# A new order for the first part of a Performer + FNet kernel: three strings that hold the order, the PSUM banks and the matmul tile forms

## The chip, the cores and the metric

One core of one Trainium2 chip. The metric is the device time of one execution in microseconds, the median of several runs. The core's engines are TensorE (PE, with its weight loads PEld), VectorE (DVE), ScalarE (ACT), GpSimd (POOL) and SyncE (SP), which here only issues DMAs. Each engine takes its instructions in the order in which the program lists them and waits on semaphores for what others have to do first.

## The reference

Two layers in a row, cut to what matters:

```python
def phi(x):                                   # q, k: (8, 8, 576, 64), omega: (128, 64)
    proj = np.einsum('bhsd,md->bhsm', x, omega)
    h = proj - np.sum(x * x, axis=-1, keepdims=True) / 2.0
    return np.exp(h - np.max(h, axis=-1, keepdims=True)) / np.sqrt(m)
q_p, k_p = phi(q * scale), phi(k * scale)
kv = np.einsum('bhsm,bhsd->bhmd', k_p, v)
z = np.sum(k_p, axis=2)
num = np.einsum('bhsm,bhmd->bhsd', q_p, kv)
den = np.einsum('bhsm,bhm->bhs', q_p, z)[..., None] + 1e-06
x = (num / den)                               # as (8, 576, 512)

u = x + np.real(np.fft.fft(np.fft.fft(x, axis=1), axis=2))
un = (u - mean(u)) / np.sqrt(var(u) + 1e-06)
out = u + np.maximum(un @ w_ch1, 0.0) @ w_ch2 # w_ch1: (512, 2048), w_ch2: (2048, 512)
```

## The kernel before, in words

**Two parts.** The first part runs the attention of all 8 batches, the Fourier mix, the residual and the conversion of the weights, and in between the plain form of the MLP for the first four blocks of tokens ("plain" blocks 0 to 3). The second part runs the MLP of all other tokens in a form with fewer multiplications, for which it needs sums of weight blocks and of token blocks made beforehand. Everything that the change touches lies in the first part.

**What the first part consists of.** Attention goes by 32 pairs of heads, n = 0 to 31, four to a batch. For each: k and q are loaded (`loads`, L497 and L501) and v (L506); PE transposes them (L642, `kqT`); PE makes the scores (`pairs`, L737); DVE takes the maximum (L679), ACT the exponent (L696); PE multiplies with v (L772, `kv`); PE transposes q's features (L642, `qeT`); PE makes numerator and denominator (L820, L828), and DVE or ACT divides (L833 to L849), which gives `x`. When four pairs of a batch are done, `mix` folds x (DVE or POOL, L873 to L915) and multiplies it with the tables cs and sn (L939, L953), ACT keeps `y` (L969), and PE multiplies it with cd and sd (L999, L1010). `residual` and `summed` (L1044 to L1066) add x and store u (L1080, L1035). The weights are loaded as `raw` (L596) into one of four slabs and converted by POOL, DVE and ACT (`narrow`, L562 to L582).

**The plain blocks** load u (`norm_of`, L1103 with its step at L1193), normalize it (DVE L1222 to L1224, POOL L1226, DVE L1228), transpose it on PE (L1233), copy it (ACT L1237, `unT`), and run the two matmuls (`plain_of`, L1299 with its step at L1287, sixteen of them, fc0 to fc15; the hidden values leave by `hidden`, L1278 to L1283; then L1324 with its step at L1309, eight of them) and store (L1334 to L1342, `rest`).

**What the first part makes for the second.** `w2_parts` (L1532 to L1579) makes the sums of w2 in seven groups, in the order 1, 2, 3, 5, 6, 4, 7. A group has four additions into the tile `sums`, the later groups four more before them into `big` (L1550, on POOL or DVE), and then five DMAs on SP that store it (L1573, L1575). A group's additions come behind the stores of the one before, by the semaphores of the same tiles. `weight_sums` (L1622 to L1628) does w1, `block_norms` (L1453 to L1484) normalizes the four blocks of tokens of the second part's first batch, i = 0 to 3, through the same `norm_of`, and adds them up (tiles `tt`, `unT`); the first matmul that reads `tt` is at L1794.

**How the order comes about.** Each of these functions is a stream (a generator) that yields a `Step` ahead of each few instructions. The step says which engines may do it, which buffers and PSUM banks it takes and gives, and what must have been listed before it. `Listing.run` holds the streams' next steps in a list, and at each turn places one of them: its instructions are emitted then and there, so the order of the turns is the order on every engine's queue. Which one is placed, and on which of its engines, is read from the string `PICKS` (one character or more for each turn). Each bank that a step takes is read from `BANKS`, and each matmul step asks `form()` for its tile form, a letter code from `FORMS` (one tile of 128 rows, or two or four tiles of 64 or 32 rows and columns beside each other). The scheduling is manual: nothing reorders the instructions afterwards.

**The chains run ahead.** Nine more pieces of work are no steps: `ahead` (L1640 to L1676) normalizes blocks of tokens for the later batches of the second part, nine chains (0 to 8) of a load on SP (L1109), statistics on ACT (L1662, L1665), three small operations on POOL (L1667 to L1669), a scaling on ACT (L1671), a transpose on DVE (L1674) and a store on SP (L1676). They go in by `BETWEEN`: after so many placed steps of the first part, such a chain is taken on by one piece. `go_on` and the planner's own search in `Listing.run` know nothing of their durations.

**Two further steps that matter below**: `warm` (L607 to L611) lets PE run six matmuls on a zeroed tile while the first loads are under way, and `first` (L617 to L622) transposes omega, which the ACT queue loads (L518), and scales it; the first scores need it.

The lines of the loop in which the order is read, and the call:

```python
        while todo:
            other, n = next(picks, (None, None))
...
            while between and between[0][0] == placed:
                next(between.pop(0)[1], None)
...
    listing.run(
        [first(), loads(), loads_v(), load_tables(), frames(), plain_norms(), mixing()]
        + [pairs(i) for i in range(NS)]
        + [w2_parts(), weight_sums(), block_norms(0, mlpp), plain(), weights(), warm()],
        picked(PICKS, 1),
        BANKS,
        betweens(BETWEEN),
    )
```

## Time and profile before

| | us |
|---|---|
| median of 3 runs | 1116.88 (1119.11, 1116.88, 1114.37) |
| the profiled execution's own time | 1114.35 |
| its span in the trace | 1112.6 |
| first part's last step on PE ends | 418.4 |
| PE busy in the span | 1093.4 |
| granted clock of PE | 1.00 |

The profiled execution is as fast as the fastest of the three runs, and its span lies 1.75 us below its own time. PE's first part ends where the program's eight last matmul steps at L1324 end and a short instruction at L2367 begins (418.37); a dozen microseconds before it everything that PE still has to do in the first part is these matmuls. How busy the engines are, stretch by stretch, and what PE waited for, is shown with the prediction.

### The profile page before, as it was taken

What the parts mean: (1) busy time and instruction counts of PE and PEld (TensorE: products, weight loads), DVE (VectorE), ACT (ScalarE), POOL (GpSimd) and SP (SyncE); (2) the same over time, 40 slices, a digit from 0 to 9 for tenths busy, and PEclk for the clock granted to TensorE, in tenths of its full rate; (3) what the DMA queues carried; (4) which work ended last, traced back from release to release, by engine and by line L of the source; (5) the groups of instructions that cost most, each with busy time, mean ns of one, the idle gap of its engine ahead of it and who ended that gap; (6) DMA issues with size and microseconds to landing.
All of it is one profiled execution on the core that took longest, in us unless ns stands there. A gap on an engine that the chain in (4) does not pass through costs nothing.

```text
span 1112.6 us, 41751 instructions
## 1 busy us (share of the span) xinstructions
PE 1093.4 (98%) x17507; PEld 934.7 (84%) x17507; DVE 885.9 (80%) x1685; ACT 539.1 (48%) x1644; POOL 390.4 (35%) x404
## 2 busy tenths in 40 slices
PE   8999999999999999999999999999999999999998
PEld 6788888878869666799998888998667999667998
DVE  6999999996676766688697777898667898668895
ACT  6998898856635464624214453223563223341221
POOL 2343443644473346634513455000365000152000
PEclk9999999999999999999999999999999999999999
DMA  7856767575675668798898768757678757556553
GB/s 230 229 183 182 241 182 220 162 212 160 221 231 187 188 169 314 236 300 287 247 303 300 211 200 260 213 155 237 206 216 262 220 154 223 167 158 220 151 158 113
DMA packets 196588, 236.77 MB, mean 213 GB/s; under 512 B 53808, under 2 KB 120624, under 8 KB 196400
## 3 DMA queue, kind: packets, MB, share of 16 engines
q1 hardware_dynamic: 195904, 233.83, 68.7%
q8 instruction: 138, 2.26, 0.9%
q14 instruction: 50, 0.41, 0.1%
q10 hardware_dynamic: 496, 0.26, 0.1%
HBM read 182.13 MB, written 56.10 MB: 214 GB/s over the span
## 4 chain that ended last, share of the span: by engine, by line
PE 90%; ACT 4%; DVE 3%; DMA 2%; issue 1%; SPq 0%; POOL 0%; DVEq 0%; ACTq 0%
PE banks L2247 30%; PE banks L1794 27%; PE banks L642 5%; PE banks L737 5%; PE banks L1324 5%; PE banks L1299 4%; PE banks L1946 4%; PE banks L772 3%; PE banks L820 2%; ACT e L696 2%; PE banks L999 1%; PE banks L939 1%; DMA kq<-in_q_dram 1%; DVE nmx L679 1%; PE banks L953 1%
## 5 line engine op out<-in xcount | busy, mean ns | idle before, releaser
L2247 PE MATMUL banks<-wl,sums 128*64 128x128 f32 x3584 | 217.5, 273 | 0.1
L2247 PEld LDWEIGHTS banks<-wl,sums 128*64 128x64 f32 x3584 | 201.6, 137 | 2.1 <-issue 0.5
L696 ACT ACTIVATE e<-banks,nmx 128x128 f32<-128x128 f32 x576 | 164.3, 426 | 21.8 <-DVE nmx L679 20.8
L679 DVE TENSOR_REDUCE nmx<-banks 128x8 f32<-128x1024 f32 (+1 forms) x96 | 89.3, 951 | 18.5 <-PE banks L737 15.4
L2247 PE MATMUL banks<-wl,hid 128*64 128x128 f32 x1536 | 99.0, 273 | 0.5 <-DVE part L2222 0.5
L2247 PEld LDWEIGHTS banks<-wl,hid 128*64 128x64 f32 x1536 | 88.0, 137 | 1.8 <-DVE part L2222 0.7
L1794 PE MATMUL banks<-unw,wxw 128*64 128x256 f32 x704 | 86.2, 379 | 0.0
L2217 ACT ACTIVATE s<-banks 128x128 f32<-128x128 f32 x112 | 30.9, 277 | 109.8 <-PE banks L2247 109.8
L737 PE MATMUL banks<-om,kqT 64*64 64x128 f32 (+1 forms) x1804 | 80.1, 276 | 2.5 <-issue 1.1
L737 PEld LDWEIGHTS banks<-om,kqT 64*64 64x64 f32 (+1 forms) x1804 | 66.2, 148 | 13.0 <-issue 4.8
L2247 PE MATMUL banks<-wl,hx 128*64 128x128 f32 x1152 | 73.6, 273 | 0.4 <-DVE part L2222 0.4
L1794 PEld LDWEIGHTS banks<-unw,wxw 128*64 128x64 f32 x704 | 53.3, 137 | 22.0
L1794 PE MATMUL banks<-rx,wxw 128*64 128x256 f32 x576 | 71.7, 379 | 0.0
L1794 PE MATMUL banks<-ttw,wxw 128*64 128x256 f32 x576 | 70.6, 379 | 0.0
L1819 ACT ACTIVATE s<-banks 128x512 f32<-128x512 f32 x65 | 38.5, 596 | 64.9 <-PE banks L1794 59.8
L2247 PEld LDWEIGHTS banks<-wl,hx 128*64 128x64 f32 x1152 | 65.4, 137 | 1.2 <-DVE part L2222 0.6
L1299 PE MATMUL banks<-unT,w 128*64 128x128 f32 (+1 forms) x720 | 64.7, 276 | 1.8 <-DVE qeT L656 1.8
L582 POOL TENSOR_TENSOR w<-w,raw 128x512 f32<-128x512 f32 x28 | 37.7, 1357 | 77.4 <-DVE raw L576 74.5
L2296 POOL TENSOR_TENSOR more<-more,part 128x512 f32<-128x512 f32 x2 | 2.7, 1336 | 172.8 <-ACT part L2289 172.8
L1299 PEld LDWEIGHTS banks<-unT,w 128*64 128x64 f32 (+1 forms) x720 | 58.6, 160 | 5.3 <-issue 2.3
L1794 PEld LDWEIGHTS banks<-rx,wxw 128*64 128x64 f32 x576 | 44.0, 137 | 17.6
L1794 PEld LDWEIGHTS banks<-ttw,wxw 128*64 128x64 f32 x576 | 44.0, 137 | 17.6
(289 smaller groups left out, 2413.3 us busy)
## 6 DMA issues: line engine op xcount, KB each, us to landing
wl<-w2l SPq DMA_DIRECT2D x245, 256.0 KB, 3.9
wxw<-w1x SPq DMA_DIRECT2D x120, 256.0 KB, 3.2
raw<-in_moe_w_ch_dram SPq DMA_DIRECT2D x32, 512.0 KB, 5.3
kq<-in_k_dram SPq DMA_DIRECT2D x32, 288.0 KB, 4.4
kq<-in_q_dram SPq DMA_DIRECT2D x32, 288.0 KB, 4.7
vd<-in_v_dram SPq DMA_DIRECT2D x32, 288.0 KB, 5.5
ur<-us SPq DMA_DIRECT2D x30, 256.0 KB, 4.6
w2l<-sums SPq DMA_DIRECT2D x14, 512.0 KB, 4.9
```

The costliest lines, as they stand in the source:

```text
L582: eng.tensor_tensor(out=dst, in0=dst, in1=lof, op=ALU.add)
L642: nc.tensor.transpose(ps[:, (j - j0) * 128 : (j - j0 + 1) * 128], src(j), ident[:])
L679: nc.vector.tensor_reduce(nmx[:, :, 0:num], pps[:, :, 0 : MF * num].rearrange("p b (c m) -> p b c m", m=MF), axis=AX.X, op=ALU.max, negate ...
L696: nc.scalar.activation(out=e[:, c + (i if num == 1 else 0), :], in_=pps[:, i, MF * c : MF * c + MF], func=AF.Exp, bias=nmx[:, i, c : c + 1],)
L737: nc.tensor.matmul(pps[cols, c, MF * m : MF * m + MF], lhsT=kqT[rows, j, cols], rhs=om2[rows, :],)
L772: nc.tensor.matmul(kvp[cols, i, 0 : D + 1], lhsT=feature(r)[rows, cols], rhs=vds[n % NV][rows, r, :], start=(r == 0), stop=(r == R - 1),)
L1299: nc.tensor.matmul(hp[cols, 0:TP], lhsT=w1[:, dc, 128 * fc : 128 * fc + 128][:, cols], rhs=unTs[key][:, dc, :], start=(dc == 0), stop=(dc ...
L1324: nc.tensor.matmul(yp[cols, 0:DM], lhsT=hs[fc][:, 128 * i : 128 * i + 128][:, cols], rhs=w2[:, fc, :], start=(fc == 0), stop=(fc == NFC - ...
L1794: nc.tensor.matmul(ps[half, span * f : span * f + span].rearrange("f (b q) -> f b q", q=Q), lhsT=left[:, P * f : P * f + P][:, half], rhs= ...
L1819: nc.scalar.activation(out=s[:], in_=ps, func=AF.Copy)
L1946: nc.tensor.matmul(cell[half].rearrange("f t (b q) -> f t b q", q=Q), lhsT=w[:, d, col : col + 128][:, half], rhs=right[:, :, d].rearrange ...
L2247: nc.tensor.matmul(ps[half, 0:128], lhsT=left[:, f][:, half], rhs=wls[head(j), i, n][:, f], start=start and f == 0, stop=(f == 3), skip_gr ...
```

## The change

Only the three strings are other ones. `BETWEEN`, and the second part's strings, stay. The diff, with the middle of each string left out:

```diff
--- before.py
+++ after.py
@@ -66,44 +66,44 @@
 
 
 PICKS = (
-    "40e0fff03eafdaege3OcdceefdcOdeccfgda37ghj0gjj7hlP79aj7ik97i8S7efhjffeHldffiehdjfdOihgihidaKedbhhciff"
-    "ecgOfeejdfdPdeeedgifdffdefd8aiii88jhd8jP8b99i8e8jcddghjgheiifcOcdciieicgPgdefJcdghbkededfgcRbggb79ij"
...
-    "accd46ddeKK72dJc7bbaa4bb9a9bc7c0777dghhdf7Bfddebd76ff1fddIe9949438686bc6aca85348dHcG7a5be957b55d1544"
-    "9Gc1F5a9a68446344584584E59189970955888574443113301110"
+    "10feeddd5dc04aa1d9bdfMefdaf983Lbdfa9gfbLP9gggcce8cifid0cIbabdgf89gbhhhfR8ehbajj8cjdeacgaja78igibbjhg"
+    "Tff68bciidTci89Ifa8bicb8ihghfjd8giigjih7gfdgffdJff9bggTiiebdck8Qigi9bbKaidi8ad9ijihgjigdjiRdjiR8bgeg"
...
+    "LLbbbLbLLa4ab3a46ba7a89a6a3bdHde6Hd4hhg6h5heiijj6g8iMi5KHa5c97f0eeagjgiiieha9e66e0N535c58cAac596c959"
+    "344ab2954b300125999a969878I952774075766652D5512321100"
 )
 
 BANKS = (
-    "0102346120164024306243643016204164024320632462014021604606245062345042604670426420340267407231640260"
-    "4524016460620240674206206415704602546064320143607264506402346234062732017426042106147026740260462462"
-    "0410652604632452017205467402624060404256174302642060245016745202642016420634520520650162505605260250"
-    "1675602501605204672016204567627450264102316742067460260462045642062637230724672402630145420640106240"
-    "5264023026731602454230412046450416725730620424670121726154305610207453"
+    "7012702452546042023645626041061424062760236424014602450246201456017420642674206204314274062354726046"
+    "2302363424020624051024614652340472601641302406274630234062704674263016724026412106141260146206404260"
+    "4710625640276701654160432406246240401625703412640764326041562042062104604276320640347606034560460543"
+    "7604634015036401604204267450142362401672363064320674624020612460262070146326547020264015640530202460"
+    "1420654675263042610216450427234501765127426205637210465314057462406257"
 )
 
 
 
 FORMS = (
-    "5W 2R W Q 2W 2Q 2W Q W Q 2W Q W C Q 3W 2R 3W 3Q W C 2W Q 3W C 2Q 2W Q W Q 3W 4Q C 2W Q 5W 3Q C W WR 3W WQ W R "
-    "2Ccz Q W 2R C 2W Q 6W C Ccz C 2R 2W R 4W 4Q W WR R 2Q 2W R W WQ W Q 2Ccz 5W 3C Ccz 3W C 2R 4W R 2W R W 2Q 3W 3R "
-    "2W 2Q 2W C Q 8W 2C R W 2R 4W Q C Q 4W 4Q WQ Q W WR R Q W Wcz 4W Wcz W 2C Ccz 8W 2Q 4W 3Q QC C Q W R RW Q czW W "
-    "Wcz 6W R W 2R czC 3C Q 9W 2R C 2R 2W Q 2W 2Q 4W WQ W 3Q 4W 2Q W QW 2W Wcz Ccz W 3C Ccz 8W 3R 5W 2R 2W 3Q 5W 3Q "
-    "5W Q 4W 3C 7W 3Q 5W 4Q QW 4W WR 3R Q Ccz czW 9W 2W 3C Ccz 9W 3Q 3W WQ 4W 3C CQ 2C 3Q 2W Ccz 5W 3Q 3C 2W C Ccz C "
-    "2R 2Q 9W 5W czC 6C 2W WQ 5C CQ W C Ccz 3C W 3C Ccz 2C Ccz 9W 3W"
+    "5W 2R 2W R 2W 2Q R W Q 2W Q 3W Q C W Q 2W Q 2W 3Q W C 2W Q 2W C W 2Q 2W 2Q 4W 3Q C Q 4W Q 3W R 2Q C W WQ 3W WQ W "
+    "R 2Ccz Q 2W 2R W Q C 6W C czC C 2R 2W R 2W Q W Q 2R W WQ 3Q 5W R WQ Q W 2Ccz 4W 2C W czC C 2W R C 4W 2R 3W 2Q W "
+    "Q 2W 2R W R W 2Q 2W C W Q 6W C W C 2Q W Q 4W Q 2C Q W C W Q 3R WQ Q QW Q W Q Ccz 6W Wcz 2C Ccz 9W 2Q W 2C 3Q CR "
+    "R C Q QW Q Ccz 2W Ccz 7W 2Q czC R 3C 2W Q 7W 2R C 2R 2W Q W 2R 5W WQ 3Q 2W R 4W Q QW 3W Wcz Ccz 3C 7W 3Q 2W Ccz "
+    "4W Q 2W 2Q C W 2Q W 2R 2Q 9W 3C 8W 3Q 6W 3R Q QW 3W WQ 4Q 2Ccz 9W 3W Q 3C Ccz 9W 6W WQ 2C 2Q QC 3C czW 3Q 9W 3Q "
+    "2C Q C Ccz 2W 3Q 9W 5W czC 9C 9C 5C CQ 4W WQ 2C 3Ccz 8W"
 )
```

The strings can't be read by eye. Decoded, that is, with each turn's stream followed in the code, they say this.

- The same 1853 turns: the same steps, each on the same engine as before. The matmul instructions of the first part (each fp32 matmul is two in the trace) become 3572 instead of 3494, by other tile forms: 38 more at L737, 8 at L1299, 12 each at L999 and L1324, 8 at L953. No other instruction is added or removed.
- The start on PE. Before: `warm`, transposes of k (n = 0, tiles 0 to 3), `first`, transposes of k and q (4 to 8), scores of n = 0. After: `first`, `warm`, transposes of k (0 to 3), transposes of k and q (4 to 8), scores of n = 0.
- The tables cs, sn, cd, sd were loaded from early on; now they stand on SP behind the loads of `raw` 8 and 9 and of v of n = 6.
- The groups of w2's sums. Before, the first group's additions stood on POOL behind the conversion of the last weights; now behind the normalization for plain block 2 (L1226), and the second group behind batch 5's last `summed` (L1062).
- The last 60 us of the first part. `n` is the position, as the time of the PE steps that come after it in the list of the first part (before and after):

| step | engine | before | after |
|---|---|---|---|
| transpose for plain block 3 (L1233) | PE | 39 | 52 |
| mix of batch 7, first half (L939) | PE | 37 | 24 |
| plain block 3, fc7 (L1299) | PE | 25 | 30 |
| transposes of u, second part's blocks 0, 1, 2, 3 (L1233) | PE | 29, 23, 17, 16 | 21, 20, 7, 10 |
| mix of batch 7, columns 0, 1, 2 (L999) | PE | 27, 20, 17 | 14, 13, 12 |
| plain block 3, last matmuls (L1324), first of eight | PE | 14 | 18 |

- The queues in that stretch, in list order. SP before: stores of groups 6 and 4, u of plain block 3, loads of chains 0 and 1, store of chain 0, stores of group 7, u of block 1, store of chain 1, loads of chains 2 and 3, u of block 0, loads of chains 4 to 6. SP after: u of plain block 3, stores of group 6, loads of chains 0 and 1, store of chain 0, stores of group 4, store of chain 1, loads of chains 2 and 3, stores of group 7, loads of chains 4 to 6, u of blocks 0 and 1.
- POOL after: additions of group 6, normalization of plain block 3, one addition of group 4, chain 0, the other additions of group 4, group 7 with chain 1 in it, `summed` of batch 6, normalization of block 0, chains 2 to 4, block 1. (Before, chain 0 stood behind all of group 4.)
- DVE after: transpose of chain 0, three additions of group 7, transpose of chain 1, divisions of n = 30 and 31 with a residual, the last addition of group 7, `rest`, the hidden values of fc0, folds of batch 7.
- ACT at the end. Before: copies `unT` of blocks 2 and 3, then the statistics and scalings of chains 7 and 8. After: statistics and scalings of chains 7 and 8, `unT` of block 3, a residual's copy, `unT` of block 2.

30 lines of the change are left out of this document (15 added, 15 removed).

## The prediction

> **What bounds the kernel now.** I read the page first, then the busy time by stretches of the first part, then what PE waited for there.
>
> ```profile
> span 1112.6 us, 41751 instructions
> PE 1093.4 (98%) x17507; PEld 934.7 (84%) x17507; DVE 885.9 (80%) x1685; ACT 539.1 (48%) x1644; POOL 390.4 (35%) x404
> ...
> PE 90%; ACT 4%; DVE 3%; DMA 2%; issue 1%; SPq 0%; POOL 0%; DVEq 0%; ACTq 0%
> ```
>
> PE is busy for 98% of the span and holds 90% of the chain that ended last: a new order can win no more than PE's idle time and can lose as much as it likes. The change touches the first part only, which ends on PE at 418.4 us (E below); the second part's order stays.
>
> ```profile
> 0.00:419.00 419.00, 405.15 (x7603) 335.30 (x7605) 344.67 (x764) 300.09 (x1051) 186.58 (x210) 1.00 0.66 200
> 0.00:20.00 20.00, 17.44 (x348) 14.30 (x349) 12.14 (x20) 13.70 (x48) 4.38 (x15) 1.00 0.96 287
> 20.00:60.00 40.00, 35.91 (x891) 30.49 (x890) 36.07 (x69) 34.87 (x132) 15.02 (x10) 1.00 0.76 215
> 60.00:120.00 60.00, 57.61 (x1234) 50.20 (x1236) 56.69 (x136) 53.60 (x190) 26.47 (x31) 1.00 0.63 189
> 120.00:320.00 200.00, 198.53 (x3824) 168.31 (x3814) 169.75 (x372) 146.53 (x522) 99.69 (x99) 1.00 0.65 199
> 320.00:360.00 40.00, 37.44 (x727) 32.81 (x726) 27.92 (x60) 19.42 (x72) 17.58 (x14) 1.00 0.59 192
> 400.00:419.00 19.00, 18.22 (x84) 9.80 (x82) 13.48 (x38) 8.75 (x20) 7.26 (x12) 1.00 0.70 192
> ```
>
> The columns are the stretch and its length, then busy us of PE, weight loads, DVE, ACT and POOL, the granted clock, the DMA share and GB/s. PE idles 419.00 - 405.15 = 13.85 us of the first part: 2.6 in the first 20 us, 4.1 from 20 to 60, 2.4 from 60 to 120, 1.5 in the next 200, 2.6 from 320 to 360, 0.8 in the last 19. DVE is 94% busy from 60 to 120, so there it limits nearly as closely as PE.
>
> ```profile
> PE banks L820 <- issue: 2.3, 2, 1.9
> PE banks L642 <- DMA kq<-in_q_dram: 1.8, 2, 1.3
> PE banks L1299 <- DVE qeT L656: 1.8, 1, 1.8
> PE banks L772 <- issue: 1.7, 3, 0.8
> PE banks L642 <- ACT e L696: 1.5, 3, 0.7
> PE banks L737 <- issue: 1.1, 2, 0.8
> PE banks L611 <- DVE ur L520: 1.0, 1, 1.0
> PE banks L737 <- ACT kv L788: 1.0, 3, 0.5
> PE banks L1233 <- DVE u L1228: 0.8, 1, 0.8
> ```
>
> Columns: total, times, longest. Of this, 2.3 + 1.7 + 1.1 = 5.1 us are "issue", waits on nothing that an order of steps can move. What an order can win back is 1.8 + 1.8 + 1.5 + 1.0 + 0.8 = 6.9 us; the 1.0 at L611 belongs to the start, counted apart.
>
> **The change, part by part.** Decoding both lists gives the same steps on the same engines; what differs is order, banks and forms. Positions in the new list are given as PE work still ahead of E ("E-30" has 30 us of PE steps behind it), from the steps' durations in the trace.
>
> *The start.* Before, PE runs the warm-up matmuls (L611) first, then the transposes of the first k (L642) and of omega (L620). After, omega's transpose comes first, and the warm-up behind it.
>
> ```profile
> 0.72 0.47 ACTq L518 DMA_DIRECT2D om<-in_omega_dram  x1
> ...
> 1.04 2.93 PE L611 MATMUL banks<-ur 128*128 128x128 f32 x12 [1.04 <-DVE ur L520]
> ...
> 3.87 0.42 PEld L642 LDWEIGHTS banks<-ident,kq 128*128 128x128 f32 x4 [0.20 <-issue]
> ...
> 4.27 0.14 PEld L620 LDWEIGHTS banks<-ident,om 128*128 128x128 f32 x1
> ...
> 5.13 0.53 PEld L642 LDWEIGHTS banks<-ident,kq 128*128 128x128 f32 x5 [0.72 <-DMA kq<-in_q_dram]
> ...
> 5.82 1.19 PEld L737 LDWEIGHTS banks<-om,kqT 64*128 64x128 f32 x20 [0.17 <-issue]
> ```
> ```profile
> DMA to landing us min/median/max: 3.2/3.2/3.2
> ```
>
> Omega is issued at 0.72 and takes 3.2 us, so it is there at 3.9. PE executes in order: it stands until 3.9, transposes (0.14), and only then spends the 2.93 us of warm-up that used to fill this wait: about 7.0. Then come 0.42 + 0.53 for the transposes of k and q and 0.17 of change-over: the first scores (L737) start at 8.1 instead of 5.82, **+2.3 us**. At the most it is 7.0 - 3.9 = 3.1; at the least 0, if what follows was waiting for later loads anyway (PE idles 2.6 us in the first 20). I take 2.3, since DVE, ACT and all their later work hang on the first scores too.
>
> A rule of the Trainium skill would add a little. The page "TensorE: Matmul & The Clock Gate", section "The HAM clock gate (the "warmup" mystery)", says that the array runs at half its clock until it has been active for a window of some 3.4 us. The granted clock is 1.00 in every stretch here, which doesn't show it, but twelve matmuls of L611 take 2.93 us, 244 ns each, and four transposes of the same size at 3.87 take 0.42, 105 ns each, which agrees. By that rule the transposes at 7.0 might still run cold; going by the 0.42 + 0.53 above, this would cost up to an estimated 1 us more, and the start would be +3.3.
>
> *Forms and banks.* The matmul instructions of the first part go from 3494 to 3572 by choice of other tile forms (two tiles of 64 rows for one of 128, and the reverse) and do the same arithmetic. Changes of the tile mode between or within steps go from 197 to 203. One costs about the 0.17 us in the row at 5.82, so six are 1.0; I take **+0.9** (0 to 1.5; the other forms' own matmuls differ by less). Banks as such issue nothing; they only decide who waits for whom, which is in the next two terms.
>
> *The middle, about 20 to 330 us.* PE's order is the same in outline with moves of a few steps, so it can remove up to the 6.9 us of hand-over waits, and can make new ones: the tables of the mix, formerly loaded early, now stand on SP behind two weight loads that wait for POOL, and the lead of some q loads shrinks. I take **-4 us**, somewhat over half of what there is to win, with -7 and +4 as ends (+4 is what the worst stretch, 20 to 60, loses now).
>
> *The last 110 us: sums for the second part.* The four additions that make each group of w2's sums (L1550) and their stores (L1571 on) form a chain of seven groups, each waiting for the stores of the one before.
>
> ```profile
> 251.17 1.26 POOL L1550 TENSOR_TENSOR sums<-w,sums 128x512 f32<-128x512 f32 x1
> ...
> 257.77 1.28 POOL L1550 TENSOR_TENSOR sums<-w 128x512 f32<-128x512 f32 x1 [5.33 <-DMA w2l<-sums]
> ```
>
> The first group's last addition ended at 252.4 (E-166), and the next had to wait 5.33 us for the stores. In the new list POOL reaches the first group only behind the normalization for the third plain block, at E-110, and the second only behind batch 5's last column, about E-93. From there the chain is rigid: four additions of 1.27 and 5.3 for the stores make 10.4 us a group, so that the groups end at E-88, -77, -67 and -57. Before the fifth can end, its queue on POOL holds a step of another chain (below) that waits for a load which SP issues only behind the fourth group's stores: E-37. The last group then ends at about E-26.
>
> *The chains run ahead (L1640 on).* The places at which their steps go into the list are fixed counts in BETWEEN, unchanged, while the steps around them moved. So SP now holds, in this order: the last group's stores, three loads of the chains, the loads of u for the first two blocks of the second part's first batch (L1103).
>
> ```profile
> 367.59 1.62 SPq L1573 DMA_DIRECT2D w2l<-big  x3
> 369.31 1.39 SPq L1575 DMA_DIRECT2D w2l<-sums  x2
> ...
> 380.11 0.36 SPq L1103 DMA_DIRECT2D u<-us  x1
> ...
> 381.92 3.68 SPq L1109 DMA_DIRECT2D kqT<-us  x8
> ...
> 386.89 1.80 SPq L1109 DMA_DIRECT2D kq<-us  x4
> ```
> ```profile
> u<-us SPq DMA_DIRECT2D x4, 256.0 KB, 4.1
> ```
> ```profile
> 384.23 0.69 DVE L1222 BATCH_NORM_STATS2 st<-u 128x6 f32<-128x512 f32 x1
> ...
> 386.86 0.54 DVE L1228 TENSOR_SCALAR u<-u,mv,rstd 128x512 f32<-128x512 f32 x1
> ```
> ```profile
> 388.68 0.66 PE L1233 MATMUL banks<-ident,u 128*128 128x128 f32 x4
> ...
> 404.64 13.90 PE L1324 MATMUL banks<-w,ht 128*128 128x512 f32 x32
> ...
> 419.83 1.04 PE L1794 MATMUL banks<-tt,w1s 128*64 128x128 f32 x16
> ```
>
> Before, the stores were out at 370.7 (E-48), u was issued at 380.11, and PE transposed it (L1233) at E-30. After: stores from E-26 for 1.62 + 1.39, three loads for 3.68 + 1.80, the issue of u 0.5, landing 4.1 and a normalization of 387.40 - 384.23 = 3.2 us: E-26 + 3.0 + 5.5 + 0.5 + 4.1 + 3.2 = E-9.7, where the new PE order asks for it at E-21.4. PE waits about **+11 us**. Within the same wait lies another: DVE's queue holds three additions of the last group, and behind them the hidden values (L1278) that free the bank for a plain matmul at E-30; those come some 4 us late, and that wait is not added, for the late u is then that much less late. Behind the waiting DVE additions also stand batch 7's last divisions and folds, which PE needs at E-24.
>
> Ends: +2, if POOL and SP run the chain much earlier than the list's places make me think; +20, if late u, the chains' steps in front of it on ACT, and the last block's sums (tt, needed at 419.83, E+1.4) add up instead of overlapping. Before, 13.9 us of plain matmuls that wait for nothing ended the first part and hid all of that; now the two last transposes of u stand inside that stretch, at E-9.5 and E-7.3.
>
> **The sum.** 2.3 + 0.9 - 4 + 11 = +10.2 us. On the profiled execution's own time, 1114.35, that is 1124.6. It was the fastest of the three runs, 2.5 us below their median of 1116.88; on the median, which the result is compared with, it is **1127**.
>
> **The rivals.**
> *Faster: the waits of the middle go and the tail holds.* The 6.9 us are gone, the start's delay falls into waits that were there, forms cost 0.9, u arrives in time: -6 us and slightly more with the 1.0 at L611, about 1110. For it: PE idles 4.1 us between 20 and 60, where the list is denser now. Against it: the chain of groups above, which starts some 60 us later and has 10.4 us a group. It decides if the last group ends before E-37, for then u is in time.
> *No change.* The tail costs only the 4 us at the bank, the middle wins 4, start and forms cost 3.2: +3, 1120. For it: POOL is only 35% busy and could catch up if the second group isn't held to E-93.
> *Much slower: the tail adds up.* Late u, then the chains' statistics on ACT ahead of the last transposes' copies (L1237), then tt late for the second part: +20 in the tail, +19 in all, 1136. For it: ACT's queue has both statistics of the last two chains ahead of those copies; against it: a PE that waits 11 us gives the others time to catch up.
> *The list isn't followed* (the order has no effect because waits decide): against it, PE, POOL, DVE and SP take their steps in list order in the trace of before, record by record.
>
> **How the numbers follow.** My forecast (1122 to 1132) has 0.45, much slower 0.18, no change 0.17, faster 0.20. Leaving out the outer half of the two extreme cases, the time lies between 1110 and 1139. Within 0.5%, 5.6 us, which is about what a measurement of this kernel can tell from no change, lies the case of no change; so faster 0.20, the same 0.17, slower 0.63.
>
> **What would show it.** The start: L620 ahead of L611, the first L737 at about 8.1. The middle: idle time of PE from 20 to 330 us below 8. The chain: L1550's second group on POOL near 325 us instead of 257.77, the last stores of w2l within 30 us of E. The tail: PE waiting for DVE u L1228 for several us, and more than 5 us idle in its last 45 us. It is wrong if the first part ends before 420 us, if w2l's stores are out by E-37, or if PE's idle time in the tail stays below 2 us.

## The result, and the profile after

The changed kernel takes 1145.83 us (median of 5 runs, 1144.90 to 1147.49); the kernel before took 1115.84 us beside it (5 runs, 1114.37 to 1119.11). The ratio is 1.0269 (95% interval 1.0248 to 1.0291): slower by some 30 us, where 10 were forecast. The profiled executions differ by 1145.4 - 1112.6 = 32.8 us of span.

The page of the changed kernel, its head and the shares of the chain of work that ended last:

```profile
span 1145.4 us, 42017 instructions
...
PE 83%; DVE 4%; ACT 3%; DMA 3%; issue 3%; POOL 2%; SPq 1%; DVEq 0%; ACTq 0%; POOLq 0%
```

PE's share of the chain fell from 90% to 83%, from some 0.90 x 1112.6 = 1001 us to 0.83 x 1145.4 = 951; what PE does no longer sets the end everywhere. POOL, which had no share, now has 2%. Busy time by stretches of the first part (columns as in the prediction: stretch, length, busy PE, weight loads, DVE, ACT, POOL, granted clock, DMA share, GB/s):

```profile
0.00:20.00 20.00, 14.00 (x246) 12.30 (x250) 8.91 (x15) 11.92 (x39) 4.28 (x15) 1.00 0.76 228
20.00:60.00 40.00, 36.71 (x972) 30.81 (x963) 38.05 (x66) 34.57 (x128) 15.28 (x10) 1.00 0.73 214
60.00:120.00 60.00, 58.34 (x1180) 50.62 (x1182) 56.36 (x140) 53.66 (x193) 25.77 (x29) 1.00 0.65 194
120.00:320.00 200.00, 197.59 (x3992) 167.45 (x3981) 169.80 (x366) 145.10 (x525) 83.43 (x86) 1.00 0.58 172
...
360.00:400.00 40.00, 31.61 (x362) 21.60 (x355) 20.62 (x49) 11.09 (x38) 23.46 (x24) 0.91 0.51 176
400.00:446.00 46.00, 37.75 (x344) 26.03 (x341) 26.43 (x71) 22.40 (x58) 15.09 (x32) 0.89 0.53 166
```

PE idles 6.0 us in the first 20 (2.6 before), 3.3 + 1.7 + 2.4 = 7.4 from 20 to 320 (8.0 before), and 8.4 + 8.2 = 16.6 from 360 to 446. The last two rows also show what no row of before did: a granted clock below 1. What PE waited for (total, times, longest):

```profile
PE banks L1299 <- ACT bmp L1048: 7.0, 1, 7.0
PE banks L1233 <- DVE u L1228: 5.7, 1, 5.7
...
PE banks L1794 <- ACT s L1819: 2.6, 1, 2.6
...
PE banks L1794 <- DVE tt L1424: 1.5, 1, 1.5
```

**Where the 32.8 us are.** For each step of PE I compare its start in the two traces at the same amount of PE work ahead of the first part's end (the sum of the durations of the steps behind it, as in the prediction's "E-30"). This delay against before is 3.2 us at E-384, 3.6 at E-180, 4.3 at E-48, 10.7 at E-36, 16.0 at E-24, 21.6 at E-21.5, 27.4 at E-17 and 26.8 at E; E is the row of L2367, 418.37 before and 445.19 now. The other 32.8 - 26.8 = 6.0 us are lost in the first rows of the second part. So: 4.3 up to the tail, 22.5 in the first part's last 48 us, 6.0 at the hand-over.

**How the tail goes wrong** is a chain over four queues. First POOL (start, duration, engine, line, operation; in brackets the idle time before it and what ended it):

```profile
326.65 1.26 POOL L1550 TENSOR_TENSOR sums<-w 128x512 f32<-128x512 f32 x1
...
365.88 1.26 POOL L1550 TENSOR_TENSOR big<-w,big 128x512 f32<-128x512 f32 x1
377.45 0.19 POOL L1667 TENSOR_SCALAR kq<-kq 128x1 f32<-128x1 f32 x1 [10.31 <-ACT kq L1665]
...
378.51 3.73 POOL L1550 TENSOR_TENSOR big<-w,big 128x512 f32<-128x512 f32 x3
...
392.49 0.19 POOL L1667 TENSOR_SCALAR kq<-kq 128x1 f32<-128x1 f32 x1
```

POOL stands still for 10.31 us inside a group of w2's sums, because chain 0's small operation (L1667) is listed behind the group's first addition and waits for its statistics, these for its load. And the load is issued late, behind the stores of the group before and six issues of other steps (365.61 to 370.52), as SP's rows show:

```profile
364.60 0.96 SPq L1575 DMA_DIRECT2D w2l<-sums  x2
...
370.63 4.87 SPq L1109 DMA_DIRECT2D kq<-us  x8
...
388.18 1.20 SPq L1080 DMA_DIRECT2D us<-x  x2
395.20 0.54 SPq L1676 DMA_DIRECT2D turned<-kq  x1
395.85 1.96 SPq L1109 DMA_DIRECT2D kq<-us  x4
397.91 1.76 SPq L1109 DMA_DIRECT2D kqT<-us  x4
...
400.65 1.57 SPq L1573 DMA_DIRECT2D w2l<-big  x3
402.32 1.19 SPq L1575 DMA_DIRECT2D w2l<-sums  x2
403.60 5.61 SPq L1109 DMA_DIRECT2D kqT<-us  x8
409.31 2.90 SPq L1109 DMA_DIRECT2D kq<-us  x4
412.26 0.90 SPq L1103 DMA_DIRECT2D u<-us  x2
```

From 389.38 (388.18 + 1.20) to 395.20 SP issues nothing: chain 1's store (L1676) is next on its queue and waits for that chain's transpose on DVE. Then come, without a pause, this store, the loads of chains 2 and 3 and two stores of other steps, and so the last group's stores begin at 400.65. They end at 403.5, and then three loads of chains pass SP, 5.61 + 2.90 us and the gap between, ahead of the two loads of u that PE needs. Rows of ACT, DVE and PE in order of time:

```profile
393.62 0.81 ACT L1671 ACTIVATE kq<-kq 128x512 f32<-128x512 f32 x1 [12.04 <-POOL kq L1669]
394.46 0.38 ACT L1048 ACTIVATE bmp<-banks 64x258 f32<-64x258 f32 x1
394.46 0.71 DVE L1674 STREAM_TRANSPOSE kq<-kq 128x512 f32<-128x512 f32 x1 [4.52 <-ACT kq L1671]
394.89 12.82 PE L1299 MATMUL banks<-unT,w 128*64 128x128 f32 x192 [7.03 <-ACT bmp L1048]
...
398.01 0.68 DVE L1550 TENSOR_TENSOR sums<-big 128x512 f32<-128x512 f32 x1
...
408.98 1.26 PE L939 MATMUL banks<-cs_sb,fold 128*64 128x160 f32 x16
...
415.13 0.69 DVE L1222 BATCH_NORM_STATS2 st<-u 128x6 f32<-128x512 f32 x1 [6.93 <-DMA u<-us]
417.75 1.11 PE L1233 MATMUL banks<-ident,u 128*128 128x128 f32 x4 [5.72 <-DVE u L1228]
...
420.29 2.08 PE L1299 MATMUL banks<-unT,w 128*128 128x128 f32 x8 [1.43 <-ACT ht L1283]
```

Chain 1's scale (ACT, L1671) waits 12.04 us for POOL. The copy of batch 6's residual (ACT, L1048) is a step that has nothing to do with chains; it stands behind that scale on ACT's queue, and frees the bank that PE's plain matmul needs: PE waits 7.03 us. DVE's transpose of the same chain waits 4.52 us too, and with it SP's store of that chain, behind which the last group's stores and then the loads of u stand: 5.72 us more on PE. The last addition of w2's sums (398.01 on DVE) also stood behind this transpose, but it was done at 398.69, before SP came to the stores.

Then the clock (columns as above):

```profile
390.00:394.00 4.00, 0.00 (x0) 0.00 (x0) 0.00 (x0) 0.38 (x1) 3.68 (x6) 0.81 0.21 62
394.00:398.00 4.00, 3.11 (x30) 3.11 (x32) 3.40 (x10) 0.82 (x2) 1.43 (x2) 0.50 0.35 97
398.00:402.00 4.00, 4.00 (x66) 4.00 (x64) 4.00 (x10) 2.21 (x7) 1.64 (x1) 0.84 0.74 227
...
418.00:422.00 4.00, 2.57 (x12) 2.17 (x11) 1.77 (x4) 3.32 (x7) 2.42 (x8) 0.50 0.32 71
```

Behind each of the two long waits PE runs at half its clock for some us: four transposes of u take 1.11 us at 417.75, and took 0.66 before. Summed over the tail's steps, the time that matmuls took above their duration of before is 5.7 us. Whether these 5.7 us are a loss of their own is tested below.

### The profile page after: what moved, and what is told of

It reads as the page before. It is cut to its first block, busy times and chain, and to the rows that moved or that the text cites. A ratio compares the mean times of both kernels' runs of the same rounds, so it can differ in the third digit from the quotient of the medians.

```text
span 1145.4 us, 42017 instructions
## 1 busy us (share of the span) xinstructions
PE 1104.1 (96%) x17663; PEld 952.6 (83%) x17663; DVE 897.4 (78%) x1685; ACT 538.3 (47%) x1644; POOL 395.0 (34%) x404
## 4 chain that ended last, share of the span: by engine, by line
PE 83%; DVE 4%; ACT 3%; DMA 3%; issue 3%; POOL 2%; SPq 1%; DVEq 0%; ACTq 0%; POOLq 0%
PE banks L2247 29%; PE banks L1794 26%; PE banks L737 4%; PE banks L642 4%; PE banks L1946 4%; PE banks L1299 3%; PE banks L1324 3%; PE banks L772 2%; PE banks L820 2%; ACT e L696 2%; PE banks L999 1%; PE banks L939 1%; POOL sums L1550 1%; PE banks L953 1%; DMA cs_sb<-k_cs 1%
## 5 line engine op out<-in xcount | busy, mean ns | idle before, releaser
L2247 PE MATMUL banks<-wl,sums 128*64 128x128 f32 x3584 | 219.2, 273 | 0.1
L2247 PEld LDWEIGHTS banks<-wl,sums 128*64 128x64 f32 x3584 | 203.4, 137 | 1.8 <-issue 0.5
L2247 PE MATMUL banks<-wl,hid 128*64 128x128 f32 x1536 | 99.6, 273 | 0.5 <-DVE part L2222 0.5
L2247 PEld LDWEIGHTS banks<-wl,hid 128*64 128x64 f32 x1536 | 88.9, 137 | 1.6 <-DVE part L2222 0.7
L1794 PE MATMUL banks<-unw,wxw 128*64 128x256 f32 x704 | 87.1, 379 | 0.0
L737 PE MATMUL banks<-om,kqT 64*64 64x128 f32 (+1 forms) x1880 | 81.5, 277 | 4.5 <-DVE kv L786 1.4
L737 PEld LDWEIGHTS banks<-om,kqT 64*64 64x64 f32 (+1 forms) x1880 | 66.8, 145 | 17.0 <-issue 5.3
L1299 PE MATMUL banks<-unT,w 128*64 128x128 f32 (+1 forms) x736 | 67.8, 286 | 9.0 <-ACT bmp L1048 7.0
L2247 PE MATMUL banks<-wl,hx 128*64 128x128 f32 x1152 | 74.8, 273 | 0.4 <-DVE part L2222 0.4
L1299 PEld LDWEIGHTS banks<-unT,w 128*64 128x64 f32 (+1 forms) x736 | 61.8, 165 | 13.7 <-ACT bmp L1048 7.3
L1794 PEld LDWEIGHTS banks<-unw,wxw 128*64 128x64 f32 x704 | 57.9, 137 | 17.5
L1794 PE MATMUL banks<-rx,wxw 128*64 128x256 f32 x576 | 72.2, 379 | 0.0
L1794 PE MATMUL banks<-ttw,wxw 128*64 128x256 f32 x576 | 71.1, 379 | 0.0
L2247 PEld LDWEIGHTS banks<-wl,hx 128*64 128x64 f32 x1152 | 66.7, 137 | 1.1 <-DVE part L2222 0.6
L1324 PE MATMUL banks<-w,ht 128*128 128x512 f32 (+1 forms) x168 | 59.2, 596 | 0.0
L1794 PEld LDWEIGHTS banks<-rx,wxw 128*64 128x64 f32 x576 | 46.9, 137 | 14.8
```

The source lines that it names most:

```text
L737: nc.tensor.matmul(pps[cols, c, MF * m : MF * m + MF], lhsT=kqT[rows, j, cols], rhs=om2[rows, :],)
L1299: nc.tensor.matmul(hp[cols, 0:TP], lhsT=w1[:, dc, 128 * fc : 128 * fc + 128][:, cols], rhs=unTs[key][:, dc, :], start=(dc == 0), stop=(dc ...
L1324: nc.tensor.matmul(yp[cols, 0:DM], lhsT=hs[fc][:, 128 * i : 128 * i + 128][:, cols], rhs=w2[:, fc, :], start=(fc == 0), stop=(fc == NFC - ...
L1794: nc.tensor.matmul(ps[half, span * f : span * f + span].rearrange("f (b q) -> f b q", q=Q), lhsT=left[:, P * f : P * f + P][:, half], rhs= ...
L2247: nc.tensor.matmul(ps[half, 0:128], lhsT=left[:, f][:, half], rhs=wls[head(j), i, n][:, f], start=start and f == 0, stop=(f == 3), skip_gr ...
```

## The experiments

Each was run beside the kernel before on the same chip; times are medians, ratios are to those runs. "Delay" is the number of the last section. Theory: late sums of w2 and the chains' places in the tail cost the time. Rivals: the head (start, forms, middle); the sums alone; the chains alone; the clock.

**1 and 2. Which end of the order costs it.** The two lists cut at 175 us of PE work ahead of E and put together crosswise, each step with its banks and form of the list that it comes from.

```diff
 h1_tail_before: the list after the change
-from E-175 on: the list after the change, chains by its counts
+from E-175 on: the list before the change, chains at their neighbours of before
 h2_tail_after: the list before the change
-from E-175 on: the list before the change, chains at their neighbours
+from E-175 on: the list after the change, chains by its counts
```

> The new order up to 175 us of PE work before the end of the first part, and from there the old order (old places of the sums of w2 and of the chains run ahead). Theory 'tail' (the loss arises in the last 60 us, out of the late sums and the chains' places): only the head's delay is left, +3.5 us on the kernel before, about 1119 to 1120, with PE's first part ending near 422. Rival 'debt' (the new middle uses up slack, and the tail only shows it): at least half of the 30 us stays, above 1130.

> The reverse: the old order up to 175 us of PE work before the end of the first part, then the new one. Theory 'tail': +26 to +29 us (30 less the head's 3.5), about 1142 to 1145. Rival 'debt': under +15, below 1131.

The new head with the old tail: 1124.40 against 1115.55 (ratio 1.0080, 1.0063 to 1.0097). The old head with the new tail: 1151.80 (1.0318, 1.0291 to 1.0344). In the first the delay is 3.3 at E-180, 7.0 behind the seam, 6.8 at E, and nothing is lost after that (span + 6.6). In the second it is -1.0 at E-180, 3.5 at E-48, 25.2 at E-17, with the same two waits, 6.2 us at L1299 for ACT's bmp and 5.3 at L1233 for u.

The tail makes the loss; the head gives some 3 us. Both kernels came out above what was expected of the theory, by 4 and 7 us, in the first by a wait that the seam itself makes (3.4 us at L737 for DVE's bmp); together they lose more than the 30 us, so the two halves are no clean sum. The loss behind E goes with the new tail too: absent in the first, 36.2 - 24.6 = 11.6 in the second. Of these 11.6 about 4 arise near 605 us, where PE waits 2.0 us for a load of weight sums (L2247), a wait that the changed kernel's profile does not have; the rest is the hand-over.

**3. Sums and chains both as before, in the new list.**

```diff
 a_both: the list after the change, except
-w2's sums and stores (L1550, L1573 on) where the new list has them
-the chains' pieces by their counts
+each of these behind the step that precedes it on its own engine in the list of before
```

> The new order with two things undone: the sums of w2 stand behind the same steps of their engines as before the change, and so do the steps of the chains run ahead; all other steps, the banks and forms stay new. Theory 'tail': the waits at the bank (7.0) and for u (5.7 + 1.4 + 0.6) go, and with them the slow clock behind them (5.7) and most of the 6.3 us at the hand-over to the second part: about -24 us against the changed kernel, 1120 to 1124. Rival 'order of the rest' (the new order of norms, folds and plain steps is what makes the tail wait): less than half of it comes back, above 1133.

It took 1160.66 (1.0408, 1.0393 to 1.0424), 15 us more than the changed kernel. That expectation failed. Its delay is 1.9 at E-180 and 32.7 at E-48, and 34.1 at E: the last 48 us lose only 1.5 instead of 22.5, as the theory has it. But 46.0 - 34.1 = 11.9 are lost behind E, which the theory had as good as gone, and the early sums now collide in the middle, where the new list has put other things in their room:

```profile
PE banks L1299 <- DVE bmp L1056: 8.1, 1, 8.1
...
PE banks L642 <- DMA kq<-in_k_dram: 6.6, 1, 6.6
```

So "the neighbours of before" is no neutral place in another list; moving work back is itself an order change.

**4. The start alone undone.**

```diff
 a_start, on PE:
-omega's transpose (L620) | warm-up (L611) | first transposes of k (L642)
+warm-up (L611) | first transposes of k (L642) | omega's transpose (L620)
```

> The new order with only the start undone: warm-up first, omega's transpose behind the first transposes of k. The prediction's term: the first scores start 2.3 us earlier, and the end comes 2.2 us earlier, about 1143.5. Rival 'hidden': the first scores start earlier, but loads or the tail's fixed waits (DMA chains that don't move with PE) eat it: within 1 us of the changed kernel, 1145 to 1146.

1144.45 (1.0254, 1.0237 to 1.0272; the changed kernel 1.0269). In the profile the delay falls from 3.2 to 0.8 at E-384 and from 26.8 to 23.4 at E, then the second part takes 2 us more, again with waits for loads of weight sums at L2247 (2.1 us). The start is worth its 2.3 us where it stands; in the time of the whole only a part can be told from the scatter.

**5, 6 and 7. Sums and chains one at a time.**

```diff
 b_sums_late: the list before the change, except
-w2's sums and stores as before
+w2's sums and stores behind the step that precedes them on their engine in the list after
 b_chains: the list before the change, only BETWEEN is another (behind the same step of its engine as after):
-    "1684016841169001690116950169501695016950171011710117101175011750217502175031762417625176361766317664"
+    "1754017541175401754117540175401754017540175411754117541175411754217543175441754517546177721777218153"
 a_chains: the list after the change, only BETWEEN is another (behind the same step of its engine as before):
-    "1684016841169001690116950169501695016950171011710117101175011750217502175031762417625176361766317664"
+    "1675016751167501675117080170801708017080173411734117341176611766217662176631772217764177651776617993"
```

(The first line of three of each; four digits are the count of steps placed, the fifth the chain. In b_sums_late the loads of u follow the last group, as their buffers demand, and the counts are shifted so that each piece of a chain keeps its neighbour.)

> The old order with one thing moved: the sums of w2 stand behind the same steps of their engines as in the new order (first group behind the normalization for plain block 2, and so on); the loads of u for the second part's first batch follow the last group, as the slabs demand. Start, middle, forms and the chains run ahead as before. Theory 'sums': this alone makes u late, PE waits some 12 to 18 us at the transposes of u (L1233) or at a bank held by a late DVE or ACT step, with some us of slow clock behind: +18 to +30, 1134 to 1146. Rival 'chains': without the chains' new places the groups close up in time: under +8, below 1124.

> The old order with one thing moved: each step of the chains run ahead stands behind the same step of its engine as in the new order. Theory 'sums': the chains alone cost little, under +5, below 1121. Rival 'chains': they are what stands in front of the divisions, folds and copies: +10 to +25, 1126 to 1141.

> The new order with only the chains run ahead undone (each of their steps behind the same step of its engine as before the change); sums late as in the new order. Theory 'sums': at most a third comes back, 1136 to 1146. Rival 'chains': 15 us or more come back, below 1131.

Late sums alone in the old list: 1155.37 against 1117.94 (1.0343, 1.0323 to 1.0363), above the 1134 to 1146 that were expected, with one wait of 18.5 us for u (below). Chains alone: 1142.88 (1.0222, 1.0203 to 1.0242), which is the rival's range, not the +5 of the theory. Either is enough for a loss of the size that both together have in the new list, 1.0269, so they don't add up; that they are two sides of one collision on SP, POOL and ACT is a reading of the waits. Behind E late sums lose nothing, and the chains alone 29.8 - 19.0 = 10.8, most of it in one wait at L1794. The two kernels' waits, sums first:

```profile
PE banks L1233 <- DVE u L1228: 24.4, 3, 18.5
```
```profile
PE banks L1794 <- ACT banks L1826: 8.6, 1, 8.6
PE banks L1299 <- DVE ht L1281: 6.6, 1, 6.6
PE banks L1233 <- DVE u L1228: 6.4, 1, 6.4
```

The third, chains put back in the new list with the sums left late, took 1140.50 (1.0209, 1.0177 to 1.0240), within the theory's 1136 to 1146. Neither the wait at L1299 for bmp nor that for u is there; the delay is 9.9 at E-48 and still 9.8 at E-17. But most of those 9.9 are a new stop: chain 0's statistics, now far ahead on ACT, wait 9.5 us for a load that SP issues behind a w2 store, and PE waits 6.0 us at L828 for ACT's qeT (L658), which stands behind them. The same mechanism, in another place. The last 17 us add 4.8 to the delay (14.6 at E) and what follows E adds 23.1 - 14.6 = 8.5.

**8 and 9. Is the half clock a loss of its own?** Extra matmuls of 128x256 in PE's two long waits keep the array busy. Their results are overwritten.

```diff
+            for _ in range({0: 30, 14: 24}.get(fc, 0) if j == NPLAIN - 1 else 0):
+                nc.tensor.matmul(psum_of(b)[:, 256:512], lhsT=w1[:, 0, 0:128], rhs=w1[:, 0, 0:256], start=True, stop=True, skip_group_check=True)
             yield Fork(hidden(fc, b, hp))
```

a_warm_half is the same with 15 and 12.

> The new kernel with 54 extra matmuls on PE that nothing uses, in two places ahead of its long waits: 30 behind the hidden values' matmul fc0 and 24 behind fc14 of plain block 3 (128x256, into columns of the step's own bank that stay unused), some 6.5 and 5.2 us of work. Theory 'clock': the waits stay, but the granted clock stays at 1.00 behind them; the slow matmuls after them (5.7 us in excess in the changed kernel's trace) go, and the time falls by 3 to 6 us, to 1140 to 1143. Rival 'work': the extra matmuls are in the way: the same time or up to 4 us more.

> The changed kernel with 15 and 12 extra matmuls of 128x256 behind the hidden values' fc0 and fc14 of the third plain block, half as many as in the run with 54: at the 0.44 us measured there they fill 6.6 and 5.3 us, just within the two waits of 7.0 and 5.7 us. Their results are overwritten by the matmuls that follow. Theory 'slow clock': the clock stays at 1.00 from 385 to 445 us, the later waits stay as they are, and the time falls by the excess occupancy of 5.7 us, with 2 to 3 us either way: 1138 to 1143. Rival: the slow clock only shortens the waits behind it (the clock drop is free): within 2 us of 1146.

The extra matmuls took twice what I had reckoned in the first kernel: 13.22 us for 30, 0.44 each. It took 1149.35 (1.0288, 1.0265 to 1.0312) with the clock at 1.00 in every stretch of the tail; its time cannot decide, since it held PE 11 us longer than the waits. The second fits the waits (6.74 and 5.34 us), and took 1152.67 (1.0311, 1.0283 to 1.0338), not the 1138 to 1143 of the theory. Its plain matmuls, at full clock throughout:

```profile
396.40 1.09 PE L1299 MATMUL banks<-unT,w 128*64 128x128 f32 x16 [0.36 <-ACT bmp L1048]
...
409.55 1.09 PE L1299 MATMUL banks<-unT,w 128*64 128x128 f32 x16 [0.94 <-DVE ht L1281]
410.48 1.26 PE L939 MATMUL banks<-cs_sb,fold 128*64 128x160 f32 x16
```

From their first row to the same step L939 they take 410.48 - 396.40 = 14.08 us; in the changed kernel, half of it at half clock, 408.98 - 394.89 = 14.09. DVE is as late as PE: PE, at full clock, waits for it in this stretch (0.40 + 0.66 + 0.94 us). The half clock is real, but behind this wait it costs nothing. Behind the wait for u the run does not decide: with PE kept busy until then, the waits for ACT's hidden values that follow grow from 1.43 + 0.57 to 1.87 + 1.48 us, and in these the clock falls all the same (0.72 from 422 to 426, 0.50 from 426 to 430). So the 5.7 us that the theory expected back did not come back, and behind the first wait the clock makes no loss by itself; behind the second that stays open. This kernel is 7 us above the changed one. Its profile shows 1.5 us of that ahead of the first extra matmul (the plain matmul before it starts at 388.33, 386.83 in the changed kernel), 2.4 at E (447.56 against 445.19), and nearly 4 near 607 us, where PE waits 2.2 us for a load of weight sums (L2249 in this kernel's file), as in experiment 2; why that load is late there was not taken apart.

**10, 11, 12. The list left alone, only the places of the chains' pieces.** If the places are the cause, some places exist under which the late sums do little harm. In the first kernel eight pieces of chains 0 and 1 stand behind the last group of sums instead of ahead of it. In the second also the loads of chains 2 to 6 stand behind the loads of u. In the third all are fitted to the gaps that the second had left.

```diff
 after the change, and then a_place01, a_places, a_places2 (first line of three)
-    "1684016841169001690116950169501695016950171011710117101175011750217502175031762417625176361766317664"
+    "1684016841169201692117340173401734117341173501735017351173511750217502175031762417625176361766317664"
+    "1684016841169201692117340173411749017491175001750117740177411774217743177441774517872178861793217943"
+    "1684016841169201692117030170611714317144171601716117330173311735017351174931749417573175741766217665"
```

> The changed kernel's list of steps, banks and forms are unchanged; only eight pieces of the first two chains run ahead stand elsewhere: both statistics (ACT) behind the divisions of pair 29, the small POOL operations, the scales and the transposes behind the last addition of the last w2 group instead of ahead of its groups, and the two stores with them. Theory 'fixed places': POOL's 10.3 us idle ahead of group 4 is gone, the last group is some 9 us earlier, ACT copies bmp (L1048) without waiting for POOL, and PE's 7.0 us wait at L1299 with the slow clock behind it falls to under 1.5. The u loads still stand behind three loads of the chains, so u comes up to 9 us earlier while PE asks for it 7 to 8 earlier: that wait stays between 2 and 7. Time 1132 to 1140, 6 to 14 below the changed kernel. Rival 'sums': the late sums by themselves hold the bank; the wait at L1299 stays over 4 us and the time is within 4 us of 1146.

> As the kernel before it in this call, and besides the pieces of chains 2 to 8 stand later: no load of a chain ahead of the loads of u for the first two blocks (they go behind the third, one behind the fourth), and their statistics, POOL operations, scales, transposes and stores correspondingly behind the steps of the second part's first norm. The steps, banks and forms are still those of the changed kernel. Theory 'fixed places': neither the 7.0 us at L1299 nor the 5.7 us at L1233 is left (each under 1.5 us), the clock stays above 0.95 in the tail, and the first part ends 15 to 22 us earlier; what ACT has to do for the chains is then packed into the last 20 us, so the hand-over to the second part may take up to 5 us more than it does now. Time 1122 to 1133. Rival 'sums': the w2 groups alone make u late; a wait of over 4 us at L1233 stays and the time is above 1138.

> Again the changed kernel's steps, banks and forms, and other places for the pieces of the chains alone, now fitted to the gaps that the last run left: the first two chains' POOL pieces between the last two w2 groups, their stores ahead of the last group's stores; loads of chains 3 and 4 in SP's gap ahead of those; loads of chains 2, 5 and 6 behind the first two loads of u; statistics, scales and transposes where ACT and DVE stood idle from 393 to 405 us, none of them ahead of the copy of y (L969) before its data are there. Theory 'fixed places': no wait of PE over 2 us is left between 370 us and the end of the first part, which ends within 8 us of the kernel before (it was 26.8); the hand-over costs under 4 us instead of 6.3; time 1120 to 1128. Rival 'sums': with sums so late some place must collide, and PE again loses over 8 us in the tail: above 1132.

The first: 1140.47 against 1116.88 (1.0198, 1.0170 to 1.0226), just above the 1132 to 1140 that were expected. The 7.0 us at L1299 are gone and the delay is 3.5 still at E-24; at E-17 it is 18.7. PE came to the transposes of u 12.4 us sooner than in the changed kernel (412.03 there, 417.75 - 5.72), and u was issued only 7.7 sooner (404.56 against 412.26), still behind three loads of chains, so the wait for u grew beyond the 2 to 7 us that were expected:

```profile
404.56 0.90 SPq L1103 DMA_DIRECT2D u<-us  x2
```
```profile
PE banks L1233 <- DVE u L1228: 10.3, 1, 10.3
```

The second: 1140.37 (1.0211, 1.0178 to 1.0243), where 1122 to 1133 was expected. Both waits are gone as the theory said (delay 5.5 at E-48, 5.7 at E-17). The end is not: I had put the statistics of chains 2 to 4 on ACT ahead of the copy of y (L969), and their loads stand on SP behind a load of u that waits for its buffer:

```profile
PE banks L999 <- ACT y L969: 6.7, 1, 6.7
```

The third: 1131.20 against 1116.09 (1.0122, 1.0095 to 1.0149); 1120 to 1128 was expected. Same steps, same banks, same forms, same engines as the changed kernel, and half of its loss is gone. The delay is 6.4 at E-48, 10.2 at E-17, 11.0 at E; the tail costs 4.6 instead of 22.5. The waits for u sum to 2.3 us; the two longest waits behind the start are those of the hand-over:

```profile
PE banks L1794 <- ACT s L1819: 2.5, 1, 2.5
PE banks L1794 <- DVE tt L1424: 2.5, 1, 2.5
```

The hand-over is still there: 17.9 - 11.0 = 6.9. This is the part that the places did not remove.

**13. The same with the start of before.**

```diff
 a_places2_start: a_places2, and on PE
-omega's transpose (L620) | warm-up (L611) | first transposes of k (L642)
+warm-up (L611) | first transposes of k (L642) | omega's transpose (L620)
```

> The kernel before it in this call, and in addition the warm-up matmuls first and omega's transpose behind the first transposes of k, as before the change. It is the best the new order can be given here. Theory: 1 to 2.5 us below the kernel before it, 1118 to 1126, still not below the kernel of before, because the head's other waits remain; rival: the start's 2.2 us are given back in later waits, as they partly were when the start alone was undone, and the two kernels are within 1 us.

1128.17 (1.0107, 1.0078 to 1.0136), where 1118 to 1126 was expected. In the profile the delay is -0.7 at E-180, 1.8 at E-48 and 4.5 at E, so up to E-180 the new order loses nothing once the start is undone. The hand-over again takes 11.4 - 4.5 = 6.9. It is the best version of the new list that I found, still above the kernel before.

## Why the prediction was wrong, point by point

The direction and the kind of mechanism were right, the size was three times as large, outside the range. What failed is the tail's term of +11: it let the pieces of the chains hold up POOL alone, which made u ready 9 us too early in the sum, and it put what comes behind u, and the hand-over, at nothing. By its own terms:

- **The start, +2.3: right.** The first L737 is at 8.06, forecast 8.1. The rows, with omega's transpose first and the warm-up behind it:

```profile
3.98 0.45 PE L620 MATMUL banks<-ident,om 128*128 128x128 f32 x1 [3.98 <-DMA om<-in_omega_dram]
...
8.06 1.16 PE L737 MATMUL banks<-om,kqT 64*128 64x128 f32 x16
```

  Undoing it (experiment 4) took 2.4 us off the delay at E-384.
- **The forms, +0.9: too small, as far as can be told.** Up to E, PE is busy for 413.30 us against 404.52. Of these 8.8 us more 5.7 are the slow matmuls; some 3 are left, for more and other matmul instructions. No run changes the forms alone.
- **The middle, -4: wrong.** Start, forms and middle were to sum to -0.8 at the tail; the delay at E-48 is 4.3, so 5.1 is missing. Of the waits that were counted as to be won (1.8 for kq's load, 1.8 for qeT, 1.5 for e), the first two are no longer among those of over 1 us, but others came: 1.4 at L737 for kv, 1.1 at L772 for v's load. The idle time from 20 to 320 us fell by 0.6 only. My test ("below 8" from 20 to 330) was a bad one: before, it was 8.0 in the 300 us of the rows, so it could not tell a gain from none.
- **The chain of groups: right in its places, late by its queues.** The second group is on POOL at 326.65, forecast near 325. The last addition was forecast for E-26, that is 392.4, and the last stores right behind it; POOL's part was over at 394.8, but the stores began at 400.65, because SP's queue held chain 1's store, which waited for the transpose until 395.20, and the loads of chains 2 and 3 ahead of them. The prediction had "a step of another chain that waits for a load" on POOL's queue; it did not follow that chain's next pieces, and the next chain's, to ACT, DVE and SP.
- **Late u, +11: the step that failed.** u was to be ready at E-9.7 = 408.7; PE transposed it at 417.75, 9.1 later. Of this 8.25 is the stores' start (400.65 against 392.4; 4.3 of these are the delay that PE had at E-48 too), 3.2 the loads of the chains (8.75 with gaps, forecast 5.5 by the rows of before), and -2.3 the landing and normalization, faster than taken. The delay went from 4.3 at E-48 to 21.6 at the transposes: 17.3 instead of 11.
- **"That wait is not added": right as a sum, wrong in its cause.** The wait for the bank was put at some 4 us, by late hidden values, and inside the wait for u. It was 7.03, and it came from ACT's copy of the residual behind chain 1's scale. PE can't pass the transposes before u is ready, whatever it waited for earlier; the two waits sum to 7.03 + 5.72 = 12.75, against 11. But they have one cause: chain 1, late behind POOL's 10.31 us, held up the bank on ACT and, on SP, everything ahead of u. SP issued nothing from 389.38 to 395.20, nearly all the time that PE stood at the bank, so u did not come nearer. In experiment 10, with these pieces out of the way, the wait for the bank is gone, u is issued 7.7 us sooner, PE waits 10.3 us for it, and the ratio falls from 1.0269 to 1.0198.
- **Behind u another 5.8 us** (delay 21.6 to 27.4), which the sum put at nothing, since "a PE that waits 11 us gives the others time to catch up": 1.43 + 0.57 of waits for ACT's hidden values, the rest matmuls at half clock. That this could be had back was not shown: of the stretch ahead of it experiment 9 showed that full clock brings nothing.
- **The hand-over, 6.0: in the bounds, not in the sum.** The upper end of the tail's term (+20) had "tt" and ACT's steps adding up. That case, the rival "much slower", was the nearer one, also in its mechanism (chains' steps on ACT ahead of the last copies L1237, then tt late; rows below). Its +20, which counted tt, stand against 22.5 + 6.0 = 28.5, and its 1136 lacked the 5 of the head as well.

The prediction's sum of 10.2 and the 32.8 measured differ by 5.1 in the head, 11.5 in the tail (6.3 up to the transposes of u, 5.2 behind them) and 6.0 at the hand-over.

The rule of the Trainium skill that was weighed for the start (page "TensorE: Matmul & The Clock Gate", section "The HAM clock gate (the "warmup" mystery)") says that the array falls back to half its clock after an idle window of about 3.4 us and needs about as long of activity to be released. I used it for the first 10 us alone. The extra 1 us that it might have added there did not come: the nine transposes behind the warm-up take 1.15 us (6.77 to 7.92), and the first scores start at 8.06, as the sum without it had it. (The 0.42 us that the prediction read for four transposes are a row of their weight loads.) The trace of the changed kernel agrees with it in the tail: PE is idle from 387.9, and the mean of 0.81 in the stretch from 390 to 394 says that the clock halved some 1.5 us before its end, 4.6 after PE stopped. By that rule alone one would add the 5.7 us of slower matmuls to the sum; experiment 9 found nothing to gain by them behind the first wait.

**What stays open.** Behind E the kernels with the new tail lose 4.8 (experiment 10) to 11.9 us (a_both), in three of them 2 to 4 us of it near 605 us for loads of weight sums; the old tail loses nothing, also with the sums late, but 10.8 with the chains at their new places. The rows of the hand-over in the changed kernel:

```profile
441.53 0.58 ACT L1237 ACTIVATE unT<-banks 128x512 f32<-128x512 f32 x1
...
448.87 1.17 SPq L1676 DMA_DIRECT2D turned<-kqT  x1
...
453.57 0.60 ACT L1819 ACTIVATE s<-banks 128x512 f32<-128x512 f32 x1 [6.08 <-DMA turned<-kqT]
```

PE's last two transposes of u end at 436.3 and 438.5; ACT copies them only at 441.53 and 442.54, behind the statistics and the scale of chain 8, and so tt is late. And ACT's first s waits 6.08 us for a chain's last store, issued at 448.87; in the kernel before, the last such store was issued at 416.58, ahead of E. In the third kernel of experiments 10 to 12 the same s waits 6.96 us for stores of batch 7 (L1035) instead. So here too it is pieces of the first part that come late in a queue; no run moves only these. Whether still better places would bring the tail's last 4.6 us was not tried. And that late sums could be had without loss at all is not shown: the best version still loses 1%.

## What to carry to other kernels

In an in-order queue a hand-placed piece of work is dangerous through what stands behind it, not through its duration: three operations of 0.2 to 0.55 us on POOL, placed by a count, held up w2's sums by 10 us, then a bank by 7 and a load by nearly 8 (experiment 10). When the order of the steps changes, counts in another string have to change with it; and when a wait is predicted, follow every piece of the same chain to the queues that it enters next, that of the DMA issues too, before calling one wait hidden in another. A wait hides in a later one only if the later one's producer goes on meanwhile; if both hang on one blocked chain, the block moves both.

## What the hardware showed unexpectedly

The granted clock falls in the middle of a kernel: to 0.50 some 4 to 5 us after PE stopped, and it was back at 1.00 in the mean of the stretch from 402 on, some 4 us after PE had started again (0.84 from 398 to 402). Behind the wait for u, with two shorter waits in between, it took until the stretch from 426 to 430 (0.93), some 9 us. A profile with one long PE wait therefore shows slow matmuls behind it, and their excess is not automatically a loss. And the extra 128x256 f32 matmuls took 0.44 us each, 13.22 for 30.
